# Sixteen or eight modes left for the end: the late rows of a spectral mix behind a sparse attention

## The chip, the cores and the metric

The kernel runs on one core of one Trainium2 chip. TensorE (PE in the profile) multiplies, and its operands are loaded by weight loads (PEld). VectorE (DVE) and ScalarE (ACT) work on what it leaves in PSUM. GpSimd (POOL) issues most transfers, SyncE (SP) those of the output. The metric is the device time of one launch in microseconds (us).

## The reference, cut to what matters

```python
# attention: 8 batches, 8 heads, 576 positions, 64 per head; heads 0..3 see the last 32
# positions, heads 4..7 every 32nd one. Its output, heads side by side, is x (8, 576, 512).
X = np.fft.rfft(x, axis=1)
Xr, Xi = (np.real(X[:, :64]), np.imag(X[:, :64]))          # 64 modes are kept
Yr = np.einsum('bmd,mde->bme', Xr, w_r) - np.einsum('bmd,mde->bme', Xi, w_i)
Yi = np.einsum('bmd,mde->bme', Xr, w_i) + np.einsum('bmd,mde->bme', Xi, w_r)
Y[:, :64] = Yr + 1j * Yi
y = np.fft.irfft(Y, n=576, axis=1)
u = x + y
out = u + np.maximum(u @ w_ch, 0.0)
```

Each of the 64 modes has its own complex 512x512 matrix, 134 MB of weights in all. They are read from DRAM once and turned into 16-bit numbers on the way (67 MB arrive in SBUF).

The inverse transform of each batch is a product of a table T (128 rows: cosine and sine of 64 modes) with the spectrum (128 x 512). The rows of T come in four groups g of 32: group g holds the cosines of modes 16g to 16g+15 and then their sines.

## The kernel before

The contraction over 512 channels is split into two halves: half 1 (the strided heads) is called slot 0 and half 0 slot 1. A "mode" below is one mode of one half, that is 128 such steps, and the weights arrive in this order, two modes (512 KB and 512 KB) to a tile, five tiles deep:

```python
SPLIT1, SPLIT0 = 56, 48
ORDER = [(1, m) for m in range(SPLIT1)] + [(0, m) for m in range(SPLIT0)]
ORDER += [(1, m) for m in range(SPLIT1, NM)] + [(0, m) for m in range(SPLIT0, NM)]
```

One mode is 16 small matmuls. Each eighth one moves its sums out of PSUM: slot 0 into Y0, slot 1, with Y0 added, into YT. The last group of slot 1 is moved in two parts, six modes and two:

```python
def mode(slot, m):
    ...
    for e in range(4):
        for c in range(4):
            nc.tensor.matmul(yv[:, mi, e, :], wt[pr, XC[c], ds(128 * e, 128)],
                             Xh[half][pr, c, :, :, m], start=(c == 0), stop=(c == 3))
    if m % 2 and (slot or m // 2 not in GUEST):
        w_fetch()                      # the next two modes into the tile that is free now
    ends = {7: 8}
    if slot and mg == 7:
        ends = {5: 6, 7: 2}
    ...
```

From a group of 16 modes follow z (the spectrum times w_ch) and y (the spectrum, turned), for four batches (a bq) at once; 32 rows of them belong to each batch:

```python
def spec_z(g, bq, zp):
    for e in range(4):
        lhs = YS["YT"][:, e, g, ds(8 * bq, 8), :].rearrange("p x m -> p (x m)")
        nc.tensor.matmul(zp, lhs, w_chs["n"][:, e, :], start=(e == 0), stop=(e == 3))

def spec_out(g, b, yp, zp):
    src, dst = ds(32 * (b % 4), 32), ds(32 * g, 32)
    act_copy(zzs[b][dst], zp[src])
    nc.vector.tensor_copy(out=yys[b][dst], in_=yp[src])
```

The early loop runs the first 48 modes of slot 1 and spreads over them the list "work" (turning x, x times w_ch), which leaves x and x·w_ch of each tile of rows in xo and v0. Groups 0 and 1 are turned into z and y here:

```python
n = 0
for m in range(SPLIT0):
    mode(1, m)
    ...                                # the next share of work
    if m >= 16 and m % 16 in (2, 4):
        spec(m // 16 - 1, m % 16 // 2 - 1)
```

Then comes the late loop over the other 24 modes. After each mode it runs one entry of the list "late": z and y of group 2 for all batches (two entries), and 20 calls of renew, which add rows 0 to 95 of the transform to v0 and xo:

```python
psum_pools(v=1, u=2)                   # one pair of banks for v, two for u

def renew(b, ts):                      # a pair of row tiles, or for ts=(4,) the last 64 rows of two batches
    vp, up = psum("v", pair=True), psum("u", pair=True)
    if n == 1:
        fill(vp[:, 0], 3)              # three matmuls whose result is not used
    for j, t in enumerate(ts):
        nc.tensor.matmul(vp[:, j], idn, v0[:, j], start=True, stop=False)
        rows_of(b, t, vp[:, j], zzs, False)      # cA[0:96] times z
    act_copy(v0, vp[:, 0:n])
    for j, t in enumerate(ts):
        rows_of(b, t, up[:, j], yys, True)       # cA[0:96] times y
    nc.vector.tensor_tensor(out=xo, in0=up[:, 0:n], in1=xo, op=AluOp.add)

rest = [(0, m) for m in range(SPLIT1, NM)] + [(1, m) for m in range(SPLIT0, NM)]
NL = len(rest) - 2
for i, (slot, m) in enumerate(rest):
    mode(slot, m)
    upto = min(len(late), i + 1)
    ...                                # late[n:upto]
    if i == NL - 1:
        v_early(0)
        u_early(0)
    elif i == NL:
        u_early(1, times=3)
```

After the last mode only group 3 (modes 48 to 63, 32 rows for each batch) is missing. The tail makes its z and y for four batches, later for the other four, and goes through 20 items: 16 with two tiles of 128 rows, 4 with the last 64 rows of two batches. For each, TensorE puts v0 and xo back into PSUM and adds the late rows, ScalarE takes the relu of v, VectorE adds u, and a transfer writes the result:

```python
def new_rows(k, acc, spectra):
    ...
        q = ds(32 * (b % 4), 32)
        nc.tensor.matmul(o, A3[q, cols], spectra[b // 4][q], start=False, stop=True)

with tc.tile_pool(name="ps_s", bufs=1, space=PSUM) as pss["s"]:
    ...
    spec_z(3, 0, zp)
    spec_y(3, 0, yp)
    act_copy(zzs[0], zp)
    nc.vector.tensor_copy(out=yys[0], in_=yp)
...
for k in range(2, LAST + 2):
    ...
    if k == 4:
        held = vps[k][:, 1]
        spec_z(3, 1, held)             # the other four batches
    if k == 5:
        held = vps[k][:, 1]
        spec_y(3, 1, held)
    ...
```

Of the kernel before, what the change touches and what calls it, by code (L numbers as in the profile page):

```python
# [56 lines left out]
def kernel(  # L57
# [89 lines left out]
    GUEST = {1: "Y0", 2: "X0", 7: "YT"}  # L147
    SPLIT1, SPLIT0 = 56, 48
    ORDER = [(1, m) for m in range(SPLIT1)] + [(0, m) for m in range(SPLIT0)]
    ORDER += [(1, m) for m in range(SPLIT1, NM)] + [(0, m) for m in range(SPLIT0, NM)]  # L150
    w_tiles = []
# [394 lines left out]
    def mode(slot, m):  # L546
        half = 1 - slot
        mi, mg = m % 8, m // 8
        if mi == 0:
            ypt[slot] = psum("y")  # L550
        yp = ypt[slot]
        yv = yp.rearrange("p (m e x) -> p m e x", m=8, e=4)
        wt = w_tiles[ORDER.index((half, m))]
        pr = ds(0, 128 if m else 64)
        for e in range(4):
            for c in range(4):
                nc.tensor.matmul(  # L557
                    yv[:, mi, e, :],
                    wt[pr, XC[c], ds(128 * e, 128)],
                    Xh[half][pr, c, :, :, m],  # L560
                    start=(c == 0),
                    stop=(c == 3),
                )
        if m % 2 and (slot or m // 2 not in GUEST):
            w_fetch()
# [3 lines that stand above are left out]
        if mi in ends:  # L569
            n = ends[mi]  # L570
            m0 = mi + 1 - n
            part = (
                slice(None),
                slice(None),
                mg // 2,
                slice(None),
                ds(8 * (mg % 2) + m0, n),
            )
            src = yp.rearrange("p (m e x) -> p e x m", m=8, e=4)[:, :, :, ds(m0, n)]
            if slot == 0:  # L580
                if m == 7:
                    spectra_tile("Y0")
                nc.scalar.activation(out=YS["Y0"][part], in_=src, func=ACTF.Copy)
            else:
                nc.vector.tensor_tensor(
                    out=YS["YT"][part], in0=src, in1=YS["Y0"][part], op=AluOp.add
                )
# [106 lines left out]
    def rows_of(b, t, acc, spectra, fresh):  # L694
        if t < 4:
            todo = [(acc, out_cols(t), b)]
        else:
            todo = [(acc[ds(64 * j, 64)], ds(512, 64), b - 1 + j) for j in range(2)]
        for o, cols, bb in todo:
            nc.tensor.matmul(  # L700
                o, cA[0:96, cols], spectra[bb][0:96], start=fresh, stop=True
            )

# [32 lines left out]
    for i, w in enumerate(first):  # L736
# [10 lines left out]
        if i == 7:  # L747
            fourier(1)
    SPLIT = [0, 2, 4, 5, 7, 8, 10]
    for b in range(B):  # L750
# [5 lines left out]
        for t in range(6):  # L756
            str_scores(b, t)
            if b > 0:
                if t < 2:
                    str_values(b - 1, 4 + t)  # L760
                elif t == 2:
                    dft(b - 1, 1)
            if t >= 2:
                str_values(b, t - 2)
            for w in front[SPLIT[t] : SPLIT[t + 1]]:
                w()
# [32 lines left out]
    actx.close()  # L799
    spectra_tile("YT")  # L800


# [3 lines left out]
    zzs = [ptr.tile([128, DM], F16, name=f"zz{i}") for i in range(B)]  # L806
    yys = [ptr.tile([128, DM], F16, name=f"yy{i}") for i in range(B)]
    w_chs["cp"] = ptr.tile([128, 4, DM], F16, name="w_cp")

# [28 lines left out]
    cA = cs["cFs"].rearrange("p a t m -> p (a t m)")[:, 0:S]  # L838
    A3 = cs["cFl"].rearrange("p a t m -> p (a t m)")[:, 0:S]

# [9 lines left out]

    def last_rows(i):
        act_copy(A3[ds(32 * i, 32)], cA[96:128])

    work.insert(8, inverse)
    for i in range(4):
        work.insert(11 + 3 * i, lambda i=i: last_rows(i))

# [6 lines left out]
    n = 0  # L864
    for m in range(SPLIT0):
        mode(1, m)
        upto = -(-len(work) * (m + 1) // SPLIT0)
        for w in work[n:upto]:
# [8 lines left out]

    def spec_late(mm, kept, eng):
        up = psum("u", pair=True)
        for bq in range(2):  # L880
            mm(2, bq, up[:, bq])
        for b in range(B):
            eng(kept[b][64:96], up[ds(32 * (b % 4), 32), b // 4])

    def fill(acc, n):
        for _ in range(n):
            nc.tensor.matmul(acc, idn, v0s[0][:, 0], start=True, stop=True)

    def renew(b, ts):
# [5 lines left out]
        vp, up = psum("v", pair=True), psum("u", pair=True)  # L895
        if n == 1:
            fill(vp[:, 0], 3)
        for j, t in enumerate(ts):
# [6 lines left out]

    def spec_last():
        spec_late(spec_y, yys, lambda o, i: nc.vector.tensor_copy(out=o, in_=i))
        fill(psum("v", pair=True)[:, 0], 5)

    late = [lambda: spec_late(spec_z, zzs, act_copy), spec_last]  # L910
    for b in range(B):
        for t in (0, 2):
            late.append(lambda b=b, t=t: renew(b, (t, t + 1)))
        if b % 2:
            late.append(lambda b=b: renew(b, (4,)))

    def units_of(item):
        P, t = item
        return [(2 * P + j, t) for j in range(2 if t < 4 else 1)]

    items = []
    for bq in range(2):
        own_t = ((0, 1, 4, 2, 3), (0, 1, 4, 2, 3)) if bq == 0 else ((0, 1, 4, 2, 3), (0, 1, 2, 3, 4))
        for ts in zip(*own_t):
            items += [(2 * bq + j, t) for j, t in enumerate(ts)]
    LAST = len(items) - 1
    vps, ups, rls, osbs = {}, {}, {}, {}

    def own(item, kept, half):
        P, t = item  # L930
        return [kept[b][:, t] for b, _ in units_of(item)] if t < 4 else [half[P]]

# [16 lines left out]
    def new_rows(k, acc, spectra):  # L949
        P, t = items[k]  # L950
        for j in range(2):
            b = 2 * P + j
            q = ds(32 * (b % 4), 32)
            if t < 4:
                o, cols = acc[:, j], out_cols(t)
            else:
                o, cols = acc[ds(64 * j, 64), 0], ds(512, 64)
            nc.tensor.matmul(  # L958
                o,
                A3[q, cols],  # L960
                spectra[b // 4][q],
                start=False,
                stop=True,
            )

    def v_done(k):
        n = len(units_of(items[k]))
        rl = ptr.tile([128, 2, 576], FP, tag=("xT", "rl")[k // 2 % 2], bufs=2, name="rl")
        rls[k] = rl[:, 0:n, 0:DM]
        vp = vps.pop(k)  # L970
        for j in [slice(0, 1), slice(1, 2)] if k == 0 else [slice(0, n)]:
            nc.scalar.activation(out=rls[k][:, j], in_=vp[:, j], func=ACTF.Relu)  # L972

    def u_done(k):
        P, t = items[k]
        up, rl = ups.pop(k), rls.pop(k)
        n = len(units_of(items[k]))
        osb = pw.tile([128, n, DM], FP, tag="w", name="osb")
        for j in [slice(0, 1), slice(1, 2)] if k == 0 else [slice(0, n)]:
            nc.vector.tensor_tensor(  # L980
                out=osb[:, j], in0=up[:, j], in1=rl[:, j], op=AluOp.add
            )
            if t < 4:
                rows = out[:, ds(128 * (t - t % 2), 256), :].rearrange(
                    "b (p i) e -> p b i e", i=2
                )
                bs = slice(2 * P + j.start, 2 * P + j.stop)
                nc.sync.dma_start(rows[:, bs, t % 2], osb[:, j])
        if t == 4:
            for j in range(2):  # L990
                (nc.scalar if j and k == LAST else nc.sync).dma_start(
                    out[2 * P + j, ds(512, 64), :], osb[ds(64 * j, 64), 0, :]
                )

    rest = [(0, m) for m in range(SPLIT1, NM)] + [(1, m) for m in range(SPLIT0, NM)]
    n = 0
    NL = len(rest) - 2
    for i, (slot, m) in enumerate(rest):
        mode(slot, m)
        upto = min(len(late), i + 1)  # L1000
        for w in late[n:upto]:
# [8 lines left out]
    with tc.tile_pool(name="ps_s", bufs=1, space=PSUM) as pss["s"]:  # L1010
        zp = pss["s"].tile([128, 512], FP, name="zp")
        yp = pss["s"].tile([128, 512], FP, name="yp")
        spec_z(3, 0, zp)
        spec_y(3, 0, yp)
        act_copy(zzs[0], zp)
        nc.vector.tensor_copy(out=yys[0], in_=yp)
    pss["v2"] = pctx.enter_context(tc.tile_pool(name="ps_v2", bufs=1, space=PSUM))

    new_rows(0, vps[0], zzs)
    new_rows(0, ups[0], yys)  # L1020
    v_done(0)
    v_early(1)
    u_done(0)
    new_rows(1, vps[1], zzs)
    v_done(1)
    new_rows(1, ups[1], yys)
    u_done(1)
    for k in range(2, LAST + 2):
        if k <= LAST:
            v_early(k)  # L1030
        if k == 4:
            held = vps[k][:, 1]
            spec_z(3, 1, held)
        if k == 5:
            held = vps[k][:, 1]
            spec_y(3, 1, held)
        if k > 2:
            u_early(k - 1)
        if k <= LAST:
            new_rows(k, vps[k], zzs)  # L1040
        if k > 2:
            new_rows(k - 1, ups[k - 1], yys)
        if k <= LAST:
            v_done(k)
        if k in (4, 5):
            act_copy((zzs, yys)[k - 4][1], held)
        if k > 2:
# [32 lines left out]
```

## Time and profile before

| | |
|---|---|
| time | 432.19 us (median of 3, 431.84 to 432.38) |
| span of the profiled run | 430.2 us |
| busy: PE, DVE, ACT, POOL | 344.0, 236.3, 203.5, 107.4 us |
| read from DRAM, written | 162.83 MB, 9.44 MB |
| mean TensorE clock granted | 0.894 of full |

Every line of the timeline gives start, duration, engine, the line of the kernel, the operation with output <- input and their shapes, a count, and in brackets the idle time before it and what ended it. Of the lines that appear below, L557 is a matmul of mode, L899 and L700 are those of renew, L243 is a copy by ScalarE, L904 the addition in renew, L676 is z and L683 y, and L935, L945, L958, L972, L980 and L988 are the steps of an item in the tail: v0, xo, late rows, relu, addition, output transfer.

### The profile page before, as it was taken

The page shows a single profiled execution, that of the slowest core. Times are in us where ns is not written, and L with a number is a line of the kernel's source. Part 1 is how long each engine was busy: PE and PEld are TensorE (multiplying, and loading weights), DVE is VectorE, ACT ScalarE, POOL GpSimd, SP SyncE. Part 2 cuts the span into 40 slices and gives each one's busy share as a digit, 9 for nine tenths or more (in the row PEclk, how much of TensorE's full clock was granted, in tenths as well). Part 3 has the DMA queues.
Part 4 walks back from the last instruction along what each step waited for, and adds up shares of the span by engine and source line. Part 5 has one row for each costly group of instructions (what it writes and reads, how often), then busy time and mean ns, then how long its engine had stood idle before and what let it go on. Part 6 is the DMA issues. An engine that isn't in the chain of part 4 may idle for free.

```text
span 430.2 us, 12274 instructions
## 1 busy us (share of the span) xinstructions
PE 344.0 (80%) x5420; PEld 238.3 (55%) x5420; DVE 236.3 (55%) x461; ACT 203.5 (47%) x357; POOL 107.4 (25%) x191
## 2 busy tenths in 40 slices
PE   2977878779988697898577767786897988888994
PEld 2865767658767575666345545454564544444331
DVE  3888778835544444534104334864684484444695
ACT  1777777634655354547131212522342463432773
POOL 8333332322432222221222221222222222210000
PEclk9999989955998889969755689999899998999998
DMA  8999999999999999999999999999999999992698
GB/s 150 213 213 213 214 214 210 212 210 212 214 213 214 214 213 214 213 214 211 214 214 214 214 213 214 213 214 213 213 213 213 214 214 214 213 206 53 223 353 304
DMA packets 30484, 91.78 MB, mean 213 GB/s; under 512 B 4000, under 2 KB 4768, under 8 KB 30432
## 3 DMA queue, kind: packets, MB, share of 16 engines
q0 software_dynamic: 24704, 81.28, 95.3%
q1 hardware_dynamic: 5216, 9.52, 6.2%
q8 instruction: 42, 0.69, 0.6%
q10 hardware_dynamic: 512, 0.21, 0.2%
q14 instruction: 10, 0.08, 0.0%
HBM read 162.83 MB, written 9.44 MB: 400 GB/s over the span
## 4 chain that ended last, share of the span: by engine, by line
DMA 69%; PE 20%; DVE 5%; issue 2%; ACT 2%; POOL 1%; DVEq 0%; ACTq 0%; POOLq 0%
DMA wt<-in_moe_w_i_dram 52%; DMA ring<-in_q_dram 7%; DMA ring<-in_v_dram 4%; DMA wt<-in_moe_w_r_dram 4%; PE y L557 3%; PE v L935 2%; PE u L945 2%; DMA ring<-in_k_dram 2%; PE v L958 1%; DVE yy L692 1%; PE sc L524 1%; PE sc L657 1%; DVE xb L233 1%; PE tp L405 1%; ACT v L243 1%
## 5 line engine op out<-in xcount | busy, mean ns | idle before, releaser
L557 PE MATMUL y<-X,wt 128*128 128x16 f16 (+1 forms) x2048 | 82.6, 193 | 37.1 <-DMA wt<-in_moe_w_i_dram 35.7
L557 PEld LDWEIGHTS <-wt 128*128 128x128 f16 (+1 forms) x2048 | 72.9, 102 | 51.4 <-issue 41.2
L178 POOL DMA_DIRECT2D wt<-in_moe_w_r_dram x62 | 36.4, 587 | 155.8 <-PE y L557 75.4
L178 POOL DMA_DIRECT2D wt<-in_moe_w_i_dram x60 | 35.4, 589 | 60.3 <-DMA wt<-in_moe_w_i_dram 49.7
L666 ACT ACTIVATE v<-sc 128x512 f16<-128x512 f32 x32 | 19.1, 597 | 64.9 <-PE sc L657 64.9
L481 ACT ACTIVATE PL<-sc 128x480 f16<-128x480 f32 (+1 forms) x48 | 27.2, 579 | 34.0 <-PE sc L467 33.7
L667 DVE COPY xo<-tp 128x512 f16<-128x512 f16 x32 | 22.1, 690 | 32.9 <-PE tp L665 32.8
L657 PE MATMUL sc<-w_cp,xT 128*128 128x512 f16 x128 | 38.3, 425 | 1.3 <-DVE xT L630 1.3
L233 DVE TENSOR_TENSOR xb<-av,rec 90x256 f16<-90x256 f32 (+2 forms) x80 | 36.0, 450 | 2.7
L232 DVE RECIPROCAL rec<-av 90x4 f32<-90x4 f32 (+2 forms) x80 | 14.6, 183 | 34.1 <-PE av L496 24.8
L412 DVE COPY qT<-tp 128x576 f16<-128x576 f16 x16 | 12.1, 758 | 33.4 <-PE tp L405 29.9
L904 DVE TENSOR_TENSOR xo<-u,xo 128x1024 f16<-128x1024 f32 x16 | 19.5, 1224 | 16.3 <-PE u L700 16.3
L243 ACT ACTIVATE v<-tp 128x640 f16<-128x640 f16 (+1 forms) x24 | 19.4, 808 | 19.0 <-PE tp L439 16.3
L405 PE MATMUL tp<-cI_s,ring 64*64 64x64 f16 x864 | 25.0, 204 | 2.0 <-issue 1.2
L370 ACT ACTIVATE PL<-sc 90x360 f16<-90x360 f32 (+1 forms) x48 | 22.8, 490 | 7.5 <-PE sc L363 7.1
L243 ACT ACTIVATE v<-v 128x1024 f16<-128x1024 f32 x16 | 16.4, 1025 | 19.4 <-PE v L700 19.3
L980 DVE TENSOR_TENSOR osb<-u,rl 128x1024 f32<-128x1024 f32 (+1 forms) x21 | 22.2, 1071 | 5.5 <-PE u L958 3.4
L451 PE MATMUL sc<-cMl_s,cI_s 128*128 128x480 f16 (+1 forms) x48 | 20.5, 426 | 3.6 <-ACT PL L481 2.0
L405 PEld LDWEIGHTS <-ring 64*64 64x64 f16 x864 | 19.5, 117 | 6.9 <-issue 2.9
L268 PE MATMUL tp<-cI_s,ring 72*128 72x72 f16 x256 | 15.3, 207 | 9.0 <-DMA ring<-in_v_dram 7.5
L972 ACT ACTIVATE rl<-v 128x1024 f32<-128x1024 f32 (+1 forms) x21 | 18.8, 902 | 6.6 <-PE u L958 4.1
L524 PEld LDWEIGHTS <-xb 108*128 108x128 f16 (+2 forms) x176 | 14.6, 103 | 11.6 <-DVE xb L233 7.1
(134 smaller groups left out, 696.2 us busy)
## 6 DMA issues: line engine op xcount, KB each, us to landing
wt<-in_moe_w_r_dram POOLq DMA_DIRECT2D x62, 512.0 KB, 18.1
wt<-in_moe_w_i_dram POOLq DMA_DIRECT2D x60, 512.0 KB, 19.4
out_dram<-osb SPq DMA_DIRECT2D x15, 512.0 KB, 3.2
ring<-in_v_dram POOLq DMA_DIRECT2D x8, 288.0 KB, 13.2
ring<-in_q_dram POOLq DMA_DIRECT2D x8, 288.0 KB, 13.6
ring<-in_k_dram POOLq DMA_DIRECT2D x8, 288.0 KB, 13.1
ring<-in_v_dram POOLq DMA_DIRECT2D x3, 512.0 KB, 14.8
ring<-in_q_dram POOLq DMA_DIRECT2D x3, 512.0 KB, 14.7
```

Source lines behind the costliest of these rows:

```text
L178: nc.gpsimd.dma_start(dst, rows)
L233: nc.vector.tensor_tensor(out=dst, in0=val.rearrange("p h (q c) -> p h c q", c=4), in1=rec[0:n, 0:pieces] .to_broadcast((n, pieces, 64)) . ...
L243: nc.scalar.activation(out=out, in_=in_, func=ACTF.Copy)
L370: nc.scalar.activation(out=PS[0:n, ds(POFF[t], 4 * n)], in_=scp[0:n, 0 : 4 * n], func=ACTF.Exp, scale=SCALE,)
L405: nc.tensor.transpose(tp[ds(64 * hp, 64), ds(64 * i, 64)], qn[ds(64 * hp, 64), ds(64 * (9 * g + i), 64)], idn[ds(64 * hp, 64), ds(64 * hp, ...
L451: nc.tensor.matmul(scp[:, 0 : n * times].rearrange("p (h x) -> p h x", h=times), idn, mask_rows("cMl", n, times), start=True, stop=False,)
L481: nc.scalar.activation(out=dst, in_=src, func=ACTF.Exp, scale=SCALE)
L557: nc.tensor.matmul(yv[:, mi, e, :], wt[pr, XC[c], ds(128 * e, 128)], Xh[half][pr, c, :, :, m], start=(c == 0), stop=(c == 3),)
L657: nc.tensor.matmul(vp, xT[:, ch], w_chs["cp"][:, ch, :], start=(ch == 0), stop=(ch == 3),)
L667: nc.vector.tensor_copy(out=xo.rearrange("p (h q c) -> p h q c", h=2, c=4), in_=tp[:, 0:512].rearrange("p (h c q) -> p h q c", h=2, c=4),)
L904: nc.vector.tensor_tensor(out=xo, in0=up[:, 0:n], in1=xo, op=AluOp.add)
L980: nc.vector.tensor_tensor(out=osb[:, j], in0=up[:, j], in1=rl[:, j], op=AluOp.add)
```

## The change

Both halves now stop at mode 56, so 16 mode steps are left for the late loop instead of 24, and eight modes (56 to 63) are missing in the tail instead of sixteen. The order in which the weights arrive changes, their number does not. What this is for: the late spectrum of all eight batches fits into 128 rows (8 batches x 8 modes x real and imaginary), so one z and one y serve all.

```diff
-    SPLIT1, SPLIT0 = 56, 48
+    SPLIT = 56
+    ORDER = [(h, m) for h in (1, 0) for m in range(SPLIT)]
+    ORDER += [(h, m) for h in (1, 0) for m in range(SPLIT, NM)]
...
+                dst = YS["YL"][:, :, :, ds(m0, n)] if mg == 7 else YS["YT"][part]
...
-                o, cA[0:96, cols], spectra[bb][0:96], start=fresh, stop=True
+            nc.tensor.matmul(o, cA[:, cols], spectra[bb], start=fresh, stop=True)
...
+    nc.vector.memset(YS["YT"][:, :, 3, :, 8:16], 0.0)
```

Modes 48 to 55 go into group 3 of the ordinary spectrum, whose other half is set to zero; renew then uses all 128 rows. Two batches share a row group of 32 in the late rows. Two tables of late rows, one for even and one for odd batches, are made with a selecting matrix, in place of four copies of T's last 32 rows:

```diff
-    def last_rows(i):
-        act_copy(A3[ds(32 * i, 32)], cA[96:128])
+    def last_rows(j):
+        lhs = pick[:, ds(16 - 16 * j, 128)]
+        for cols in (ds(0, 512), ds(512, 64)):
+            ap = psum("sc")[:, 0 : cols.size]
+            nc.tensor.matmul(ap, lhs, cA[:, cols], start=True, stop=True)
+            act_copy(AL[j][:, cols], ap)
```

The early loop has 56 modes for the same work and makes z and y of group 2 as well. The late list keeps its 20 calls of renew, without the unused matmuls; z and y of group 3 (modes 48 to 55) come as two entries, for four batches each:

```diff
-    def spec_late(mm, kept, eng):
+    def spec_early(bq):
         up = psum("u", pair=True)
-        for bq in range(2):
-            mm(2, bq, up[:, bq])
-        for b in range(B):
-            eng(kept[b][64:96], up[ds(32 * (b % 4), 32), b // 4])
-    def fill(acc, n):
...
+        spec_mm(3, bq, up[:, 1], up[:, 0])
+        for b in range(4 * bq, 4 * bq + 4):
+            spec_out(3, b, up[:, 1], up[:, 0])
...
-        if n == 1:
-            fill(vp[:, 0], 3)
...
-    rest = [(0, m) for m in range(SPLIT1, NM)] + [(1, m) for m in range(SPLIT0, NM)]
+    rest = [(slot, m) for slot in range(2) for m in range(SPLIT, NM)]
...
-        upto = min(len(late), i + 1)
+        upto = min(len(late), -(-len(late) * (i + 1) // NL))
```

The tail makes z in two halves of 256 columns, y once, and neither again later. It has 18 items: 16 pairs of batches b and b+2, and two that hold the last 64 rows of four batches:

```diff
+    items = [
+        ((b, b + 2), t)
+        for b0 in (0, 1)
+        for t in range(4)
+        for b in (b0, b0 + 4)
+    ] + [(range(b, b + 4), 4) for b in (0, 4)]
...
+            q = ds(32 * (b // 2), 32)
...
+                o, AL[b % 2][q, cols], spectra[q], start=False, stop=True
...
-        spec_z(3, 0, zp)
-        spec_y(3, 0, yp)
-        act_copy(zzs[0], zp)
+        lhs = [YS["YL"][:, e].rearrange("p x m -> p (x m)") for e in range(4)]
+        for h in (ds(0, 256), ds(256, 256)):
+            for e in range(4):
+                nc.tensor.matmul(
+                    zp[:, h], lhs[e], w_chs["n"][:, e, h], start=(e == 0), stop=(e == 3)
+                )
+            act_copy(zzs[0][:, h], zp[:, h])
...
-        if k == 4:
-            held = vps[k][:, 1]
-            spec_z(3, 1, held)
-        if k == 5:
-            held = vps[k][:, 1]
-            spec_y(3, 1, held)
```

## The prediction

> **What bounds the kernel now.** I read the chain that ended last first, then the slices, then the stretch from 340 us to the end in the timeline. Two thirds of the chain are weight transfers:
>
> ```profile
> DMA 69%; PE 20%; DVE 5%; issue 2%; ACT 2%; POOL 1%; DVEq 0%; ACTq 0%; POOLq 0%
> DMA  8999999999999999999999999999999999992698
> ```
>
> The second line is the busy share of the transfer engines in 40 slices of 10.8 us. They are full until slice 36, where the last weights land, so up to some 390 us no work on an engine sets the time. After that they are nearly empty, and then busy with the output. The table by stretches (PE, PEld, DVE, ACT, POOL busy, clock, transfer share, GB/s) dates it:
>
> ```profile
> 380.00:385.00 5.00, 4.15 (x48) 2.15 (x47) 1.92 (x2) 1.78 (x3) 1.03 (x2) 1.00 1.06 211
> 385.00:390.00 5.00, 4.59 (x62) 2.81 (x60) 2.89 (x3) 2.76 (x3) 0.00 (x0) 1.00 0.73 146
> 390.00:395.00 5.00, 4.32 (x40) 2.08 (x39) 1.94 (x3) 0.75 (x2) 0.00 (x0) 1.00 0.24 47
> 395.00:400.00 5.00, 4.10 (x39) 1.68 (x36) 2.27 (x4) 2.44 (x4) 0.00 (x0) 1.00 0.00 0
> ...
> 410.00:415.00 5.00, 5.00 (x33) 1.57 (x32) 4.71 (x5) 3.91 (x5) 0.00 (x0) 1.00 1.01 376
> ```
>
> So there are three regimes: weights at 213 GB/s to about 390, a gap to 400, the output at up to 380 GB/s to the end. The question is what ends the second. The timeline shows the late loop waiting for weights at first, and no more at its end:
>
> ```profile
> 358.79 0.65 PE L557 MATMUL y<-X,wt 128*128 128x16 f16 x16 [1.00 <-DMA wt<-in_moe_w_i_dram]
> ...
> 383.30 0.64 PE L557 MATMUL y<-X,wt 128*128 128x16 f16 x16 [0.85 <-DMA wt<-in_moe_w_i_dram]
> ...
> 385.92 0.38 PE L899 MATMUL v<-v,cI_s 128*128 128x512 f16 x1 [0.20 <-ACT v L243]
> ...
> 386.99 1.02 ACT L243 ACTIVATE v<-v 128x1024 f16<-128x1024 f32 x1 [1.12 <-PE v L700]
> ...
> 388.06 0.38 PE L899 MATMUL v<-v,cI_s 128*128 128x512 f16 x1 [0.20 <-ACT v L243]
> ...
> 391.61 0.60 ACT L243 ACTIVATE v0h<-v 128x512 f16<-128x512 f32 x1 [1.45 <-PE v L700]
> ...
> 395.86 1.04 PE L676 MATMUL zp<-w_ch,YT 128*128 128x512 f16 x4 [0.39 <-DVE YT L585]
> ```
>
> The reader is to see a closed loop: there is one pair of banks for v, so TensorE fills it (385.92 to 386.96), ScalarE empties it (386.99 to 388.01), and only then the next fill may start (388.06). One renew of two tiles costs 2.14 us, with a mode's matmuls in the shadow of ScalarE's copy. A pair of modes arrives each 4.92 us (378.45 to 383.30 and so on), 2.46 us for one. At one renew per mode the loop is just fast enough.
>
> **What the skill says.** "PSUM — Partial Sum Buffer", section "Summary: rules for kernel authors", tells one to read another bank than the one being written. The code has no other bank for v, and the trace agrees: fill and copy alternate. "ScalarE: Activation LUTs", section "What ACT_TABLE_LOAD costs", gives 186 ns plus 0.833 ns for each element of a partition; for 1024 that is 1.04 us and for 512 0.61, and the trace has 1.02 and 0.60. A copy of only 32 rows is no cheaper in the trace: eight of 32x512 take 4.80 us from 341.93 on, 0.60 each. "TensorE: Matmul & The Clock Gate", section "Wait — 56ns, not 53.3ns?", gives 215.7 ns for 512 columns on the full clock and 426.7 on half of it; in the trace such matmuls start 0.22 us apart, and around 360 us, where the clock dips, 0.43.
>
> **The change part by part.** I number the mode steps by their place in the order of weights, 0 to 127. The weights are the same, so place 112 (with 113) still arrives for 358.79.
>
> 1. Early loop. The same work goes over 56 modes instead of 48; PE is at most 4.8 of 5 us busy there now, so this only relaxes it. The selecting matmuls, their four copies and the memsets lie under the transfers. Nothing gained or lost: 0 us.
>
> 2. Late loop. It started at place 104 (339.13) and starts at place 112. Its list is as long: 16 renews of two tiles, 4 of the last rows, 2 entries for z and y. Instead of 22 entries over 22 modes (54 us of weights) it has 22 over 14 (34 us). That is 1.57 entries for each mode, some 3.2 us of work, per 2.46 us of weights. It falls behind, and no wait for weights remains. So I add durations:
> - first mode 358.79 + 0.65 = 359.44;
> - first z and y: z is ready for ScalarE 1.12 us after its start (395.86 to 396.98), four copies of 32x512 at 0.60 take 2.4, then the first v copy 1.02: 359.44 + 4.5 = 363.9;
> - 15 more renews of two tiles x 2.14 = 32.1;
> - 4 renews of last rows. At 379.58 their first matmul after the unused ones starts, ScalarE runs from 380.34 to 380.94, the next fill is at 380.99: 1.4 each, 5.6;
> - second z and y: ScalarE takes four copies more (2.4), partly under matmuls, but a fill waits for its rows; I take 2.4.
>
> The sum is 363.9 + 32.1 + 5.6 + 2.4 = 404.0. I add 0.5 for a clock dip like that at 360 us. The last copy of the late loop thus ends at 404.5; now it ends at 391.61 + 0.60 = 392.2. That is **12.3 us later**. Taking the unused matmuls out saved 4 x 0.65 us, which is in the sum.
>
> 3. From there to the start of the last z nothing is changed: v0 and xo of item 0, two modes, three rounds of xo of item 1, the sums of the last two modes. It took 395.86 - 392.2 = 3.65 us and takes that again, because it was not waiting for weights.
>
> 4. Start of the tail. z comes in two halves, so ScalarE starts after four matmuls of 256 columns: zz ready some 1.5 us after the start instead of 1.72. Gain 0.2.
>
> 5. Items. In the middle of the tail an item takes 1.297 us (eight additions in 10.37 us), on PE and DVE alike. Now the additions run from 398.69 to 425.55, 26.9 us. After the change: item 0 in two pieces 1.3, items 1 and 2 begin as now (the third item of now starts at 401.80, 3.1 after the first), then 16 x 1.297 = 20.75, and about 1.0 because an item of four batches needs eight matmuls of late rows instead of four. That is 24.9, 2.0 less: the second z and y and the four half-filled items (three gaps of 0.6 to 1.0 us around 403, 406 and 407) fall away. But the 9.4 MB need 24.8 us at 380 GB/s, the engines already are full from 410 to 428 us, and the last two items issue eight transfers of 128 KB, each taking some 0.55 us of the queue, six of them on one queue. I take 0.7 us of the gain for that: **2.2 - 0.7 = 1.5 us less**.
>
> Span: 430.2 + 12.3 - 1.5 = 441.0. The median lies 1.99 above this span (432.19 against 430.20), so about 443; with a second spec entry that hides better, 442. I say **442.5 us**, 2.4% more.
>
> **The rivals.**
> - The weights hide it. If the late loop kept up, the last z would start as now or 2 us earlier, at the landing of the last weights, and the tail's gain of 1.5 to 3 us would remain: 427 to 431 us. The 1.00 and 0.85 us of waiting for weights speak for slack, but they sum to 4.1 us over the whole late loop, and about 20 us of weight time are taken away from it. The 54 us less 34 against 45 us of work decide against it.
> - Only part of the list falls behind. TensorE runs in program order, so a renew cannot pass a waiting mode, and none can be made earlier since all of them now use modes 48 to 55 of both halves, the last of which is at place 111. I see no such part; it would give 436 to 439.
> - Output as the new bound. If the transfers take the tail's gain wholly, 444; if the tail starts without its gaps and saves 3.5 us, 440.
> - The late loop becomes worse than the sum: ScalarE's copies of the first z and y wait for one another, the clock dips as around 360 us for longer: 445 to 447.
>
> **Range and chances.** The 2.14 and 1.4 us are read off the same code; an error of 0.1 us in each gives 2 us. The z and y entries are uncertain by 1 us each, the tail by 1.5. Together some 3.5 us: 438 to 446.5. Two per cent slower is 440.8, less than my number by half of that spread: slower 0.68, same 0.28, faster 0.04.
>
> **What would show it.** In the profile of the changed kernel: place 112 again at about 358.8 with a wait for weights, none after it in the late loop; fills following ScalarE's copies at 2.14 us; the last v0h copy near 404.5; the transfer share falling to nothing between about 392 and 412 us, a gap of 20 us instead of 8; the last z near 408; from it to the end 32.5 to 33 us instead of 34.3. If modes 57 to 61 of slot 1 still wait for weights, or the last z starts before 400, step 2 is wrong. If the tail takes 31 us or less, step 5 is too small.

## The result, and the profile after

The changed kernel takes **456.2 us** (median of 6, 452.49 to 458.38) against 432.13 before: 1.055 times as long, 95% interval 1.050 to 1.060. I had said 442.5 and 438 to 446.5. The direction was right; the loss is 24 us where I saw 10.

The profiled execution is the quickest of the six, span 450.7 us. In the lines of the changed kernel, L677 and L684 are the matmuls of z and y (L1017 those of the last z), L693 is the copy of y, L910 and L701 are the matmuls of renew, L915 is its addition, and L658 and L631 belong to the early work (x times w_ch, and a copy of the turned x). Its chain and the transfer engines' slices, from its page:

```profile
DMA 44%; PE 31%; DVE 12%; ACT 8%; issue 3%; POOL 1%; DVEq 0%; ACTq 0%; POOLq 0%
DMA  8999999999999999999999999999999999600498
```

The share of transfers in the chain has fallen from 69% to 44%, and two slices (of 11.3 us) between weights and output are now empty, where none was before. The same from its table by stretches (PE, PEld, DVE, ACT, POOL busy, clock, transfer share, GB/s):

```profile
385.00:390.00 5.00, 4.34 (x52) 2.23 (x49) 2.60 (x3) 2.76 (x5) 0.00 (x0) 1.00 0.98 196
390.00:395.00 5.00, 1.71 (x21) 0.95 (x19) 3.30 (x4) 2.46 (x4) 0.00 (x0) 0.68 0.23 45
395.00:400.00 5.00, 4.54 (x28) 1.79 (x26) 1.92 (x2) 2.05 (x2) 0.00 (x0) 0.63 0.00 0
400.00:405.00 5.00, 4.32 (x41) 2.11 (x41) 2.47 (x4) 2.08 (x3) 0.00 (x0) 1.00 0.00 0
...
425.00:430.00 5.00, 5.00 (x33) 1.54 (x32) 4.78 (x4) 4.00 (x4) 0.00 (x0) 1.00 0.99 366
```

The weights end at about 393 us, some 1 us earlier than before. What lies between them and the output is the late loop, as predicted. But two numbers were not predicted: the clock of 0.68 and 0.63, and PE busy for only 1.71 of 5 us from 390 to 395. The timeline shows what TensorE waited for there:

```profile
387.05 1.02 PE L677 MATMUL u<-w_ch,YT 128*128 128x512 f16 x4
...
388.34 0.58 ACT L243 ACTIVATE zz<-u 32x512 f16<-32x512 f32 x1 [0.49 <-PE u L684]
388.95 0.68 DVE L693 CAST yy<-u 32x512 f16<-32x512 f32 x1 [1.59 <-ACT zz L243]
...
389.67 0.59 ACT L243 ACTIVATE zz<-u 32x512 f16<-32x512 f32 x1 [0.75 <-DVE yy L693]
...
390.29 0.69 DVE L693 CAST yy<-u 32x512 f16<-32x512 f32 x1 [0.65 <-ACT zz L243]
...
392.35 0.59 ACT L243 ACTIVATE zz<-u 32x512 f16<-32x512 f32 x1 [0.76 <-DVE yy L693]
392.96 1.02 ACT L243 ACTIVATE v<-v 128x1024 f16<-128x1024 f32 x1
...
394.04 0.59 PE L910 MATMUL v<-v,cI_s 128*128 128x512 f16 x1 [3.29 <-ACT v L243]
```

These are the copies of z (ScalarE) and y (VectorE) of four batches. The brackets name the other engine each time: the copies take turns, although z and y lie in different banks. Both banks belong to one tile, `up`. TensorE stands idle for 3.29 us, and the matmul after it takes 0.59 instead of 0.38. In the kernel before, where z and y of the late entries lie in two tiles, eight copies of each ran side by side:

```profile
341.93 4.80 ACT L243 ACTIVATE zz<-u 32x512 f16<-32x512 f32 x8 [2.36 <-PE u L676]
...
342.85 5.61 DVE L907 CAST yy<-u 32x512 f16<-32x512 f32 x8 [2.97 <-PE u L683]
```

In numbers, the sum of the prediction against the profile:

| | predicted | measured |
|---|---|---|
| place 112 runs at | 358.79 | 360.51 |
| first late entry | 359.44 | 361.46 |
| late list, from there to the end of its last copy | 45.1 | 51.9 |
| last copy to last z | 3.65 | 3.70 |
| last z to the first addition | 2.6 | 3.26 |
| last z to the end (34.3 before) | 32.8 | 33.6 |
| span | 441.0 | 450.7 |

### The profile page after: what moved, and what is told of

Same layout as the page of the kernel before. It is cut to its first block, busy times and chain, and to the rows that moved or that the text cites. A ratio compares the mean times of both kernels' runs of the same rounds, so it can differ in the third digit from the quotient of the medians.

```text
span 450.7 us, 12277 instructions
## 1 busy us (share of the span) xinstructions
PE 353.2 (78%) x5419; PEld 243.1 (54%) x5419; DVE 242.3 (54%) x470; ACT 205.7 (46%) x362; POOL 107.5 (24%) x191
## 4 chain that ended last, share of the span: by engine, by line
DMA 44%; PE 31%; DVE 12%; ACT 8%; issue 3%; POOL 1%; DVEq 0%; ACTq 0%; POOLq 0%
DMA wt<-in_moe_w_i_dram 39%; ACT v L243 4%; PE y L557 4%; DMA wt<-in_moe_w_r_dram 4%; PE v L910 2%; DVE xb L233 2%; DVE kz L275 2%; DVE yy L693 2%; PE v L941 2%; PE v L701 2%; PE u L951 2%; PE sc L524 2%; PE tp L405 2%; PE y L524 2%; PE sc L658 1%
## 5 line engine op out<-in xcount | busy, mean ns | idle before, releaser
L557 PE MATMUL y<-X,wt 128*128 128x16 f16 (+1 forms) x2048 | 82.7, 192 | 37.1 <-DMA wt<-in_moe_w_i_dram 35.9
L658 PE MATMUL sc<-w_cp,xT 128*128 128x512 f16 x128 | 39.8, 435 | 2.5 <-DVE xT L631 2.4
L915 DVE TENSOR_TENSOR xo<-u,xo 128x1024 f16<-128x1024 f32 x16 | 19.6, 1225 | 15.3 <-PE u L701 15.3
L451 PE MATMUL sc<-cMl_s,cI_s 128*128 128x480 f16 (+1 forms) x48 | 21.5, 449 | 2.5 <-ACT X L243 1.6
L524 PEld LDWEIGHTS <-xb 108*128 108x128 f16 (+2 forms) x176 | 15.9, 109 | 12.1 <-DVE xb L233 6.8
L910 PE MATMUL v<-v,cI_s 128*128 128x512 f16 x32 | 13.5, 421 | 10.7 <-ACT v L243 9.7
```

What stands on the lines that cost most here:

```text
L524: nc.tensor.matmul(xp[:, ds(192 * cp, 192)].rearrange("p (f m) -> p f m", f=3), xb[b][0:n, base + t, ds(128 * cp, 128)], F[0:n, :, t, :], ...
L658: nc.tensor.matmul(vp, xT[:, ch], w_chs["cp"][:, ch, :], start=(ch == 0), stop=(ch == 3),)
```

## The experiments

Times are medians of all executions, ratios are against the kernel before on the same chip; the columns from the first late entry to the span come from the one profiled execution of each version. "List" is the time from the first late entry to the end of the last v0h copy.

| run | first late entry | list | last z | first addition | span | time | ratio |
|---|---|---|---|---|---|---|---|
| before | 339.94 | 52.3 | 395.86 | 398.69 | 430.2 | 432.1 | 1 |
| changed | 361.46 | 51.9 | 417.07 | 420.33 | 450.7 | 456.2 | 1.055 (1.050 to 1.060) |
| two tiles | 362.98 | 44.6 | 411.21 | 414.47 | 445.3 | 447.1 | 1.034 (1.032 to 1.036) |
| before, late list | 359.25 | 48.0 | 410.92 | 413.75 | 445.8 | 447.6 | 1.036 (1.034 to 1.037) |
| early pace | 358.85 | 53.2 | 415.70 | 418.96 | 449.3 | 451.1 | 1.045 (1.041 to 1.049) |
| whole z | 364.12 | 52.0 | 419.71 | 422.54 | 453.0 | 454.6 | 1.051 (1.049 to 1.053) |
| warm early | 362.68 | 44.6 | 410.96 | 413.79 | 444.1 | 446.3 | 1.032 (1.027 to 1.038) |
| no group 2 | 359.16 | 44.6 | 407.34 | 410.70 | 441.3 | 443.3 | 1.025 (1.023 to 1.028) |
| single banks | 362.60 | 35.9 | 400.04 | 403.64 | 433.8 | 435.9 | 1.008 (1.006 to 1.009) |
| before, single | 339.22 | 54.9 | 395.15 | 398.75 | 430.7 | 433.9 | 1.004 (1.003 to 1.005) |
| before, single, filled | 339.86 | 52.0 | 395.61 | 400.30 | 432.6 | 434.4 | 1.006 (1.004 to 1.007) |
| single, paced | 359.03 | 36.8 | 397.24 | 400.42 | 430.9 | 433.6 | 1.004 (1.002 to 1.006) |

**Two tiles.** z and y in tiles of their own, the only edit:

```diff
-        up = psum("u", pair=True)
-        spec_mm(3, bq, up[:, 1], up[:, 0])
+        zp, yp = psum("u", pair=True)[:, 0], psum("y")
+        spec_mm(3, bq, yp, zp)
...
-            spec_out(3, b, up[:, 1], up[:, 0])
+            spec_out(3, b, yp, zp)
```

> The changed kernel, with z and y of modes 48 to 55 in two PSUM tiles instead of the two halves of one. Theory A (ScalarE's four copies of z and VectorE's four of y take turns because they read one tile, and TensorE then stands idle over 3 us, so that its clock falls): the copies run side by side, each of the two entries ends 2.5 us earlier, the half-clock fills after them go (2.5 us in all), the last z starts near 409.5 instead of 417.1 us, and the time is 445 to 449 us. Rival B (the copies take turns for another reason, or the time is ScalarE's in any case): last z near 417, 453 to 458 us.

447.1 us, and the list takes 44.6 us. In its timeline the copies run side by side, and the next fill comes after only 1.15 us of idle time of TensorE, on the full clock:

```profile
364.10 2.40 ACT L243 ACTIVATE zz<-u 32x512 f16<-32x512 f32 x4 [1.50 <-PE u L677]
364.34 2.81 DVE L693 CAST yy<-y 32x512 f16<-32x512 f32 x4 [1.42 <-PE y L684]
...
366.52 1.02 ACT L243 ACTIVATE v<-v 128x1024 f16<-128x1024 f32 x1
...
367.60 0.38 PE L910 MATMUL v<-v,cI_s 128*128 128x512 f16 x1 [1.15 <-ACT v L243]
```

So theory A holds. The last z came at 411.2, not 409.5, because this execution began its list 1.5 us later still. The four executions lie within 1.5 us (446.26 to 447.75), those of the changed kernel within 5.9: the half-clock stretches and the spread went together, but there is no trace of the slower executions.

**Before, late list.** The other part alone: the kernel before, with its late entries held back to place 112.

```diff
-        upto = min(len(late), i + 1)
+        upto = max(0, min(len(late), -(-len(late) * (i - 7) // (NL - 8))))
...
-        if n == 1:
-            fill(vp[:, 0], 3)
...
-        fill(psum("v", pair=True)[:, 0], 5)
```

> The kernel before, in its own order of modes, but with all 22 late entries begun only at place 112 (14 modes) as in the changed kernel, and without the unused matmuls. It has z and y in two tiles. Theory A (the late list is too long for 14 modes of weights, whatever else is changed): first renew ends near 367, last copy of the late loop 404 to 406, last z near 408 to 409, 444 to 447 us. Rival C (the weights hide a late list of 45 us, and what costs is the tail or the copies): last z at 395 to 398, 431 to 435 us.

447.6 us: rival C falls. The compressed list alone costs 15.3 us (432.3 for the kernel before on this chip), with the old order, the old tail and z and y in two tiles. It is somewhat more than expected, and the list takes 48.0 us. For the larger part this is the clock: TensorE has had next to nothing to do from 340 to 358 us and begins on half of it. Its first eight z matmuls take 3.23 us, in the kernel before 1.90, and two of the first renews take 2.7 instead of 2.14.

```profile
358.77 0.64 PE L557 MATMUL y<-X,wt 128*128 128x16 f16 x16 [3.87 <-DMA wt<-in_moe_w_i_dram]
359.25 3.23 PE L676 MATMUL u<-w_ch,YT 128*128 128x512 f16 x8
```

**Early pace.** The early loop's work over 48 modes instead of 56, in the changed kernel:

```diff
-        upto = -(-len(work) * (m + 1) // SPLIT)
+        upto = min(len(work), -(-len(work) * (m + 1) // 48))
```

> The changed kernel, with the work of the early loop spread over 48 of its 56 modes instead of all, so that it is done before place 112 comes. Theory A (the late loop began 2 us late, at 361.5, because the early loop's last entries and the z and y of group 2 ran past the landing of place 112, with a lower clock): first late entry at 359.4 to 359.8, everything after it 2 us earlier, 452 to 455 us. Rival D (the start is set by something else): first late entry at 361 to 362, no difference.

The list begins at 358.85, 2.6 us earlier than in the changed kernel, as theory A has it. The median, 451.1 us, is 5 less, below the 452 to 455 expected; the profiled executions differ by only 1.4. Not all of the early start stays: TensorE is idle so much before that the clock is at half from 345 to 360 us, and the first copy of v comes only 1.6 us earlier.

**Whole z.** The last z in one piece of 512 columns again:

```diff
-        for h in (ds(0, 256), ds(256, 256)):
+        for h in (ds(0, 512),):
```

> The changed kernel, with the last z in one piece of 512 columns as before. Theory A (the second half of z waits for ScalarE's copy of the first, because both are one tile, and so halving costs): from the start of the last z to the first addition 2.8 us instead of 3.26, the time 0.4 us less, not to be seen in the total. Rival E (halving helps as meant): 3.5 us or more.

From the last z to the first addition 2.83 us instead of 3.26: halving costs, as theory A has it. In the changed kernel the matmuls of the second half carry a wait for ScalarE's copy of the first:

```profile
417.07 0.61 PE L1017 MATMUL zp<-w_ch,YL 128*128 128x256 f16 x4 [0.39 <-DVE YL L586]
417.77 0.38 ACT L243 ACTIVATE zz<-zp 128x256 f16<-128x256 f32 x1 [4.40 <-PE zp L1017]
418.20 0.60 PE L1017 MATMUL zp<-w_ch,YL 128*128 128x256 f16 x4 [0.52 <-ACT zz L243]
```

The two halves are not only one tile but also one bank of 512 columns; no run here tells which of the two makes them wait. The total (454.6 against 456.2) cannot show 0.4 us under a spread of several.

**Warm early.** Why did the list begin late? Two tiles and whole z, and unused matmuls after each of the last 20 modes of the early loop:

```diff
+        if m >= 36:
+            fp = psum("sc")
+            for _ in range(4):
+                nc.tensor.matmul(fp, idn, v0s[0][:, 0], start=True, stop=True)
```

> The changed kernel with z and y of the late entries in two tiles and the last z in one piece, and with four matmuls whose result is not used after each of the modes 36 to 55 of the early loop. Theory F (with the work spread over 56 modes TensorE has so little to do there that its clock falls to half around 340 to 355 us, and so the work runs past the landing of place 112 and the late loop begins at 361.5 to 363): the clock stays at 1.0 from 340 on, the first late entry begins by 360, 2 to 3 us earlier than with two tiles alone, and the time is 443 to 445 us instead of 447.1. Rival G (it begins late because the entries before it are too many for their modes at any clock): the added matmuls make it begin later, 447 us or more.

Theory F falls: the clock is at 1.0 in every stretch from 335 us on, and the list begins at 362.68 all the same.

```profile
345.00:350.00 5.00, 5.00 (x64) 3.29 (x63) 3.63 (x7) 2.95 (x5) 1.18 (x2) 1.00 1.06 213
350.00:355.00 5.00, 4.76 (x44) 2.50 (x41) 3.50 (x7) 2.25 (x4) 0.71 (x2) 1.00 1.07 215
355.00:360.00 5.00, 5.00 (x61) 3.11 (x60) 3.21 (x5) 2.49 (x5) 0.47 (x1) 1.00 1.07 214
```

The time, 446.3 us, fits neither forecast. The added matmuls fill TensorE, though, so this did not show that the clock has no part in it; the next run does.

**No group 2.** Two tiles, and the two calls that make z and y of modes 32 to 47 in the early loop left out (their rows are set to zero, so a part of the result is missing; only the times are read):

```diff
-        if m >= 16 and m % 16 in (2, 4):
+        if 16 <= m < 48 and m % 16 in (2, 4):
```

> The changed kernel with z and y of the late entries in two tiles, and WITHOUT the two calls that make z and y of group 2 (modes 32 to 47) in the early loop; those rows are set to zero, so this leaves part of the result out and only its times are read. Theory N (the late loop begins at 361.5 to 363 instead of 359.4 us because these two calls, after modes 50 and 52, take TensorE and hold VectorE's queue for four copies each): the first late entry begins at 359.0 to 360, some 3 us earlier than with two tiles alone (362.98), the time is 443.5 to 445 us. Rival G (the ordinary entries of the early loop are too many for its last modes): it begins at 362 or later, 446 us or more.

The list begins at 359.16, and place 112 waits for its weights again, as in the kernel before:

```profile
358.68 0.64 PE L557 MATMUL y<-X,wt 128*128 128x16 f16 x16 [1.68 <-DMA wt<-in_moe_w_i_dram]
```

So the late start comes with these two calls (after modes 50 and 52), which the change moved out of the late loop into the last modes of the early one. The trace of the changed kernel shows how: the first call's four copies of y occupy VectorE until 351.33, a copy of the early work stands behind them, and TensorE waits for that copy:

```profile
348.54 2.79 DVE L693 CAST yy<-tp 32x512 f16<-32x512 f32 x4 [0.56 <-PE tp L684]
...
352.12 0.82 PE L658 MATMUL sc<-w_cp,xT 128*128 128x512 f16 x3 [1.96 <-DVE xT L631]
```

Without the calls this wait is gone. It needs the early work beside it, too: in the early-pace run, where the calls stay and the work is done before them, the start is on time as well. The clock is no explanation: it is 0.62 and 0.70 from 340 to 350 us in the run without the calls, and the start is on time. With both faults of the changed late loop taken away the time is 443.3 us, and the list 44.6 us long.

**Single banks.** If fill and copy of v take turns, a second bank should shorten the list itself. All tiles of the late loop become single banks:

```diff
-    psum_pools(v=1, u=2)
+    psum_pools(lv=2, lu=4)
...
         for j, t in enumerate(ts):
-            nc.tensor.matmul(vp[:, j], idn, v0[:, j], start=True, stop=False)
-            rows_of(b, t, vp[:, j], zzs, False)
-        act_copy(v0, vp[:, 0:n])
+            vp = psum("lv")
+            nc.tensor.matmul(vp, idn, v0[:, j], start=True, stop=False)
+            rows_of(b, t, vp, zzs, False)
+            act_copy(v0[:, j], vp)
```

(u likewise; z and y of the late entries get single banks too; v0 and xo of items 0 and 1 are put into PSUM after the last y, and the last z is in one piece.)

> The changed kernel with all tiles of the late loop single banks (two for v, four for u and for z and y), so that ScalarE empties one bank of v while TensorE fills the other; the last z is in one piece, and v0 and xo of items 0 and 1 go into PSUM after the last y instead of before the last modes. Theory A (the late loop is too long because fill and copy of v take turns, 2.14 us for a pair): a pair takes 1.3 to 1.7 us, the list ends near 397 instead of 413, the last z is near 398 to 400, and the time is 432 to 436 us. Rival H (ScalarE, VectorE or TensorE itself is the bound, and the wait for the bank hides it): 2.0 us or more for a pair, 445 us or more.

435.9 us, 20 us less than the changed kernel; about 10 of them are those of two tiles and the whole z, which this run contains (446.3 with these in the warm-early run). The list takes 35.9 us. Two renews, one followed by a mode and one not:

```profile
367.01 0.38 PE L701 MATMUL lv<-zz,cFs_s 128*128 128x512 f16 x1
367.28 0.38 PE L910 MATMUL lv<-v,cI_s 128*128 128x512 f16 x1
367.42 1.09 ACT L243 ACTIVATE v<-lv 128x512 f16<-128x512 f32 x2 [0.19 <-PE lv L701]
...
368.77 1.09 ACT L243 ACTIVATE v<-lv 128x512 f16<-128x512 f32 x2 [0.27 <-PE lv L701]
...
370.50 1.08 ACT L243 ACTIVATE v<-lv 128x512 f16<-128x512 f32 x2 [0.64 <-PE lv L701]
```

ScalarE starts a pair after 1.35 us and, with a mode in between, after 1.73, instead of 2.14; between the copies it now waits for TensorE, which is the bound.

**Before, single.** The same banks in the kernel before, without its unused matmuls, and with the same later place for items 0 and 1.

> The kernel before with the same single banks in its late loop, and without the unused matmuls. Theory A: its late list already had slack to some 383 us, so only the last five entries gain; the last modes are done when their weights have landed, the last z begins at 393 to 395 instead of 395.9, and the time is 429 to 431.5 us. Rival H: 432 us or more.

433.9 us, no gain (1.004), where 429 to 431.5 was expected. TensorE now waited 7.7 us for weights in the late loop instead of 4.1, and the clock was 0.50 in all stretches from 384 to 392 us.

**Before, single, filled.** The same, with unused matmuls in those waits, and xo of item 1 put into PSUM later:

```diff
         mode(slot, m)
+        if i % 2 and i < 20:
+            fill(psum("lv"), 5)
```

> The kernel before with single banks in its late loop as in the run before it, but with five matmuls whose result is not used after each second mode of the late loop up to the twentieth, and with xo of item 1 put into PSUM after the first late rows. Theory A with theory K (single banks alone won nothing because TensorE then waited 7.7 us for weights instead of 4.1 us and its clock fell to half from 383 to 392 us): the clock stays at 1.0, the last z begins at 393 to 394.3 instead of 395.2, and the time is 429 to 431.5 us. Rival L (the time is set by the landing of the last weights and the output, not by the clock): 432 us or more.

The clock stays at 1.0 to 395 us, but the last z comes hardly earlier than in the kernel before (395.61 against 395.86) and the time is 434.4. Theory K falls, rival L holds. The reason is in the timeline, at the last two modes:

```profile
391.21 0.60 ACT L243 ACTIVATE v0h<-lv 128x512 f16<-128x512 f32 x1 [0.82 <-PE lv L700]
...
392.16 0.64 PE L557 MATMUL y<-X,wt 128*128 128x16 f16 x16 [0.77 <-DMA wt<-in_moe_w_i_dram]
394.59 0.64 PE L557 MATMUL y<-X,wt 128*128 128x16 f16 x16 [1.79 <-DMA wt<-in_moe_w_i_dram]
395.61 1.89 PE L676 MATMUL zp<-w_ch,YT 128*128 128x512 f16 x4 [0.39 <-DVE YT L585]
```

The list is done, and the last mode waits for its weights until 394.59. In the kernel before it ran without a wait for weights:

```profile
394.88 0.59 PE L557 MATMUL y<-X,wt 128*128 128x16 f16 x16
```

That is 0.29 us later than here, and its last load had been issued 0.27 us earlier (383.44 against 383.71). If the load takes as long, that kernel was within some 0.6 us of its weights to the very end, and its late loop only just kept up. Here the last z, after the wait of 1.79 us, runs on half the clock (1.89 us instead of 1.04), and the first addition comes 4.7 us after its start instead of 2.8.

**Single, paced.** Single banks in the changed kernel, the early work over 52 modes, xo of item 1 later.

> The changed kernel with single banks, the work of the early loop spread over 52 of its 56 modes, and xo of item 1 put into PSUM after the first late rows. Theory A: the late loop begins near 359.5 instead of 362.6, its rate stays at 1.3 to 1.8 us for a pair, the last z is near 397.5 instead of 400.0, the first addition 2.9 us after it instead of 3.6, and the time is 432 to 434 us: what is left of the loss is a list of 35 us in 34 us of weights, after a start at place 112. Rival M (the list is at its end bound by something that the start does not move): last z at 399.5 or later, 435 us or more.

433.6 us, last z at 397.24: as expected, rival M falls; only the first addition comes 3.2 us after the last z instead of 2.9. The list begins at 359.03 and takes 36.8 us, so its last copy ends at 395.8. The last load, issued at 383.35, lands 9.6 us later, so the list ends 2.8 us after the weights. The tail from the last z takes 33.7 us. No version here has a lower median than the kernel before.

## Why the prediction was right or wrong

**What bounds the kernel: right about the loop, not quite about its end.** The late loop of the kernel before waits for weights up to 383.30, and from there fill and copy of v do take turns. But "no more at its end" was too simple: going by the filled run, the last mode could have run at most some 0.6 us earlier, so loop and weights end almost together.

**Step 2, the core of it: right.** Place 112 sets the earliest start, and no wait for weights remains: from 361 to 418 us TensorE waits 10.6 us for the copy of v, and never for a weight. The term for the list was 45.1 us with the allowance for the clock, 44.6 without; with z and y in two tiles the list measures 44.6, in three runs. This is no cancelling of errors: in the first of these runs the first entry with its copy of v takes 4.56 us (4.5 in the sum), the second adds 2.36 (2.4), and a pair takes 2.14. The kernel before with the list held back shows the cost without the rest of the change. The first rival (the weights hide it) is refuted. (The pair of modes that I named, 378.45 to 383.30, is 4.85 us apart, not 4.92; over the five pairs from 358.79 it is 4.90. For 14 modes this is 0.1 us.)

**Where it failed: step 2's terms for z and y.** I took "four copies of 32x512 at 0.60 take 2.4" for each of the two entries: ScalarE's alone, as if VectorE's ran beside them, which they do in the kernel before. In one tile they took turns: the two entries lasted 2.5 us (361.46 to 368.46, 7.0 for 4.5) and about 2.4 us longer. Both times TensorE then stood idle for 3.3 us and went on at half its clock: three renews took 2.97, 2.97 and 2.94 us instead of 2.14, 2.5 us in all, where I had allowed 0.5. The two-tile run takes all three off: 51.9 - 44.6 = 7.3 us. My fourth rival had named this very thing, copies that wait for one another and a longer clock dip, but for the first entry only and at 445 to 447 us; what it leaves out is the second entry and the late start.

**Step 1: failed.** "Nothing gained or lost: 0 us." It cost 2.0 us in the profiled execution. I looked at TensorE's load, not at VectorE's queue, nor at where the moved z and y of group 2 fall: in the last six modes, with early work still to do and no time after it. TensorE's wait of 1.96 us for VectorE is the size of the loss. The run without the two calls begins the list at 359.16.

**Step 3: right**, 3.70 us for 3.65.

**Step 4: wrong in sign.** Halving z cost 0.4 us instead of gaining 0.2, because its second half waited for the copy of the first.

**Step 5: right in direction, with two sizes off that nearly cancel.** The additions take 24.3 us (predicted 24.9, before 26.9). From the last addition's end to the end of the span 6.1 us pass instead of 4.65: 1.45 us lost where I took 0.7. That this is due to the eight small transfers, six of them on one queue, was not tested. Together with step 4 the tail is 0.8 us longer than predicted.

The sum closes: 2.0 + 2.5 + 2.4 + 2.5 - 0.5 in the late loop and 0.8 in the tail are 9.7 us, which is 450.7 - 441.0. What stays open is the rest of the difference between 442.5 and 456.2 us: the median of the executions is 3.7 us above the profiled one, whose granted clock was also the highest of the six (0.863; the others 0.840 to 0.858).

## What to carry to other kernels

Before leaving less input time for the same late work, add that work up: a list of 45 us cannot hide in 34 us of weights, and what does not fit lies on the path. Results that two engines are to take out of PSUM together belong in two tiles, as here, not in two halves of one; the timeline shows whether their copies overlap. And a loop whose mean load leaves room can still be late at its end, where there is no time left to catch up.

## What I had not expected of the hardware

TensorE's clock fell to half after waits much shorter than 3 us. In the kernel before with single banks it came to 0.50 (the number before the last two of each line) after two stretches in which TensorE was busy 1.41 and 1.04 of 2 us, with one wait of 1.55 us in them:

```profile
380.00:382.00 2.00, 1.41 (x10) 0.43 (x6) 1.03 (x3) 1.09 (x2) 0.52 (x1) 1.00 1.08 217
382.00:384.00 2.00, 1.04 (x18) 0.76 (x19) 0.52 (x1) 0.00 (x0) 0.52 (x1) 0.69 1.05 209
384.00:386.00 2.00, 2.00 (x7) 0.64 (x5) 0.23 (x1) 1.20 (x2) 0.00 (x0) 0.50 1.07 209
```

With five unused matmuls in each pair of modes the clock stayed at 1.0 to 395 us; those of the kernel before may serve the same end, which no run tested alone. The busy share does not decide it: in the two-tile run TensorE was busy 3.17 of 5 us from 365 to 370 and the clock stayed at 1.0. These runs give no rule for when it falls.

The last weights come more slowly than the rest: from 389 to 392 us those of the kernel before arrive at 98 to 115 GB/s instead of 213, with a transfer share near 0.5, though all loads had been issued by 384 us. The changed kernel shows 94 to 102 GB/s in the same way from 390 to 392. Whether this is because the last four modes are loaded one at a time, or because few loads are left, was not tried.
